# Windowed attention and a gated expert on one core: h by Strassen's algorithm from the fourth chunk on

## The chip, the core and the metric

The kernel runs on one core of a Trainium2 chip. A core has five engines with queues of their own: PE (TensorE, matrix multiplication), DVE (VectorE), ACT (ScalarE), POOL (GpSimd) and SP (SyncE, which here issues nearly all DMA transfers). The profile shows PE's weight loads apart, as PEld. The metric is the time of one execution on the device in microseconds (us).

## The reference

What is computed is an attention with a mask, whose result goes through an expert with a gate:

```python
scores = scale * np.matmul(q, k.transpose(0, 1, 3, 2))      # batch 8, 8 heads, 576 positions, 64 wide
# heads 0-3: the last 32 positions; heads 4-7: every fourth of the last 128
scores = np.where(masks[None, :, :, :], scores, -1000000000.0)
attn = np.exp(scores - np.max(scores, axis=-1, keepdims=True))
attn = attn / (np.sum(attn, axis=-1, keepdims=True) + 1e-09)
x = np.matmul(attn, v)                                     # then as 4608 tokens x 512

h = x @ w_in                                               # 512 -> 2048
sp = np.maximum(h, 0.0) + np.log1p(np.exp(-np.abs(h)))
g = h * erf(sp)
out = g @ w_out                                            # 2048 -> 512
```

The weights come as numbers of 64 bits. The kernel splits each factor of the two expert products into a high and a low part of 32 bits (type fp32r), and forms every product as three: high x high, high x low, low x high.

## The kernel before, in words

**Attention** works on 72 units of 256 queries by two heads. A unit is visited twice: its scores, mask and maximum at one visit; three units later its transposes (`turn`), its product with the values (`values`) and the writing of its rows as high and low part (`rows_hi` on ACT, `rows_lo` on DVE). Finished rows go to DRAM tiles `xT` and come back as chunks. The first 14 units run alone, the others beside the expert.

**The expert** takes the 4608 tokens in nine chunks of 512 (0 to 8), and h in pairs of 128 columns. A step t (of 72) is a pair in a chunk; 8 steps make a chunk, only chunk 0 is worked in two halves around chunk 1. A step is two half-steps, x = 2t + j, with j 0 or 1. In each, `mm1` makes 128 columns of h for the chunk's 512 tokens: 12 matmuls (4 parts of the 512 inner numbers, three products each) of a 128x128 weight by 512 tokens, into one PSUM bank `h`. DVE copies the bank to `hc` (`take`, L492). When both columns of a pair are there, ACT computes the argument (sigmoid and logarithm, `argument`) and a half-step later erf (`table`); DVE multiplies and splits g into `ghi` and `glo` (`gate`, j = 0 for the product and the first half, j = 1 a half-step later for the second). `mm2` for the step two back, 12 matmuls of 512 columns into four PSUM banks `acc`, stands on PE behind each `mm1`.

**The order** is written by hand: the loop over x at the end of the kernel issues everything, and no scheduler moves it. On PE a half-step is: the transposes of a visit if there is one, `mm1`, `mm2`, then values and scores of the visit. On DVE: `take`, copies of transposes, normalizing, `gate`, mask and maximum, `rows_lo`. `visits()` is the table that says at which x which units are visited; from unit 30 on they come in twos. SP issues DMAs strictly in the order of the program, and an issue that waits holds up those behind it. PSUM is full: `h`, two banks for scores and transposes (`sp`), one (`tx`) for the values' products and four `acc`.

**SBUF** holds both parts of both weights for the whole run (`win_hi`, `win_lo`, `wout_hi`, `wout_lo`), made in the first half-steps; four tiles `xs` hold a chunk's x, with two of the staging tiles `dbl` in turn with them for every second chunk.

Of the kernel before, what the change touches and what calls it, by code (L numbers as in the profile page):

```python
# [10 lines left out]
F32 = mybir.dt.float32  # L11
# [7 lines left out]
P = 128  # L19
# [54 lines left out]


def visits():
# [12 lines left out]
    return at  # L89
# [39 lines left out]
def attn_moe_kernel(ctx: ExitStack, tc: tile.TileContext, qk, v, masks, eye, w_in, w_out, out):  # L129
# [15 lines left out]

    win_hi = wpool.tile([P, CC, DF], F32R, name="win_hi")
    win_lo = wpool.tile([P, CC, DF], F32R, name="win_lo")
    wout_hi = wpool.tile([P, FT, DM], F32R, name="wout_hi")
# [9 lines left out]
    vz = [one.tile([P, SIDE, 2, D], F32, name=f"v{i}") for i in range(2)]  # L158
    pz = [one.tile([P, TOK], F32, name=f"pT{i}") for i in range(2)]

# [8 lines left out]
    def place(u, p):  # L169


        if u < FREE:
            return acc[(u + 1 + 2 * p) % 4][:, p * P:(p + 1) * P]
        at = p * PARTS * P + (u in second) * P
        return (spb[1] if p else bank)[:, at:at + P]

# [187 lines left out]
    for g in range(DF // TOK):  # L364
        cs = slice(g * TOK, (g + 1) * TOK)
        for c in range(CC):
            prep.append((USED[2 * g], w_in[c, g], win_hi[:, c, cs], win_lo[:, c, cs]))
    for f in range(FT):
# [23 lines left out]
    def load_w(i):  # L392
        if prep:
# [3 lines left out]
            staged.append((i, d, hi, lo))  # L397

    calls = [0]

    def prep_act():


        calls[0] += 1
        if made:
            w, hi, lo = made.popleft()
            nc.scalar.copy(out=hi, in_=w)
            rest.append((calls[0], w, hi, lo))
        if staged:
            i, d, hi, lo = staged.popleft()  # L410
            w = io.tile([P, TOK], F32, name="w", bufs=4)
            nc.scalar.activation(out=w, in_=d[:, :, 1].bitcast(F32), func=AF.Abs, scale=REBASE)
            begun.append((calls[0], i, d, hi, lo, w))

    def prep_dve(keep=None):
# [3 lines left out]
        if rest and rest[0][0] < calls[0]:  # L419
            _, w, hi, lo = rest.popleft()  # L420
            nc.vector.tensor_tensor(lo, w, hi.bitcast(F32), op=ALU.subtract)  # L421
        if begun and begun[0][0] < calls[0]:
# [51 lines left out]
    def mm1(t, j):  # L474
# [7 lines left out]
        for k, cc in enumerate(ccs):  # L482
            for i, (w, x) in enumerate(((win_hi, hi), (win_hi, lo), (win_lo, hi))):
                nc.tensor.matmul(h, w[:, cc, ft * P:(ft + 1) * P], x[cc],  # L484
                                 start=(k == 0 and i == 0), stop=(k == CC - 1 and i == 2))

    hs, ls, gs = {}, {}, {}
# [79 lines left out]
    with tc.manual_schedule():  # L567
# [25 lines left out]
        for x in range(2 * (NT + 2)):  # L593
# [8 lines left out]
            if t < NT:  # L602
                after = STEPS[t + 1][0] if ends(t) and t + 1 < NT else None
                if x == 2 * HALF - 4:
                    load_x(1, range(twice))
                elif after and after > 1 and j == 0:
# [3 lines left out]
                mm1(t, j)  # L610
                if x == 0:
                    for a in stores:
                        store_x(*a)
                if after is not None and j == PAIR - 1:
                    load_x(after, range(twice, CC))
                    hold(False)
                take(t, j)

# [130 lines left out]
```

## Time and profile before

| | |
|---|---|
| median of 3 runs | 926.96 us (926.67 to 928.45) |
| profiled execution, first to last instruction | 924.6 us |
| PE busy | 895.2 us, 97% |
| PE matmuls | 8208, each with its own weight load |
| DVE, ACT, POOL busy | 561.4, 638.2, 75.4 us |
| moved by DMA | 103.66 MB, mean 112 GB/s |
| chunk 3's first half-step (x = 48) starts | 345.3 us |
| chunk 8's last half-step of h starts | 903.9 us |

The span is 2.4 us under the median of the runs. A row of groups reads: line, engine, operation, what is written <- what is read, shapes, count, then total busy time and the mean of one in ns, then the idle time of the engine ahead of it with what ended it. A row of the timeline reads: start, duration, engine, line, operation, tiles, count. The end of a matmul is modelled, so its pace is read from starts.

### The profile page before, as it was taken

To read this page: it belongs to the slowest core of one execution; us is meant where nothing else is said; L and a number is where in the kernel's file an instruction comes from. 1 tells how busy PE (TensorE), PEld (TensorE's weight loads), DVE (VectorE), ACT (ScalarE), POOL (GpSimd) and SP (SyncE) were. 2 spreads that over 40 slices of the span, in tenths; PEclk is the share of its full clock that TensorE was granted. 3 is DMA by queue.
4 is the path that set the end of the run, shared out by engine and by line. 5 is a ranking of instruction groups with operands and counts; after the bars stand their busy time and mean duration, and the time that the engine had idled before them with its cause. 6 is when DMAs were issued, how large, how long until landed. Compare 5 with 4: busy or idle time off the path is not lost.

```text
span 924.6 us, 20394 instructions
## 1 busy us (share of the span) xinstructions
PE 895.2 (97%) x8208; PEld 730.8 (79%) x8208; DVE 561.4 (61%) x1633; ACT 638.2 (69%) x1266; POOL 75.4 (8%) x92
## 2 busy tenths in 40 slices
PE   4689999999999999999999999999999999999998
PEld 3467877888888888888888888888888888888886
DVE  6879989886566655555566555555655444445444
ACT  7779988885866866766678675877676554455553
POOL 2211100000001100000000010000000000000000
PEclk9999999999999999999999999999999999999999
DMA  8885544532632252324233263233311311011001
GB/s 300 271 280 186 170 161 141 164 120 92 213 119 73 75 170 81 108 74 145 71 118 100 71 216 100 95 103 111 120 50 38 117 51 41 1 45 46 1 1 45
DMA packets 53823, 103.66 MB, mean 112 GB/s; under 512 B 7136, under 2 KB 20192, under 8 KB 53728
## 3 DMA queue, kind: packets, MB, share of 16 engines
q1 hardware_dynamic: 53440, 101.83, 33.0%
q8 instruction: 64, 1.05, 0.5%
q10 hardware_dynamic: 288, 0.52, 0.1%
q14 instruction: 31, 0.25, 0.1%
HBM read 74.15 MB, written 27.26 MB: 110 GB/s over the span
## 4 chain that ended last, share of the span: by engine, by line
PE 90%; DVE 5%; ACT 2%; DMA 2%; issue 1%; SPq 0%; POOL 0%; DVEq 0%; ACTq 0%
PE h L484 42%; PE acc L525 40%; PE tx L262 3%; PE sp L204 3%; PE sp L243 1%; DMA dbl<-in_w_in_dram 1%; DVE w L426 1%; DVE w L427 1%; DMA qk<-in_qk_dram 1%; PE sp L262 1%; DVE win_lo L421 1%; DVE prob L215 0%; DVE w L425 0%; DVE s L507 0%; DVE x L309 0%
## 5 line engine op out<-in xcount | busy, mean ns | idle before, releaser
L492 DVE COPY hc<-h 128x512 f32<-128x512 f32 x144 | 99.4, 691 | 273.1 <-PE h L484 273.0
L484 PE MATMUL h<-x,win_hi 128*128 128x512 f32 x832 | 260.7, 395 | 2.1 <-DVE hc L492 1.9
L525 PE MATMUL acc<-wout_hi,ghi 128*128 128x512 f32 x576 | 227.6, 395 | 0.4 <-DVE ghi L510 0.2
L525 PE MATMUL acc<-wout_lo,ghi 128*128 128x512 f32 x576 | 224.6, 390 | 0.0
L496 ACT ACTIVATE s<-hc 128x1024 f32<-128x1024 f32 x72 | 76.4, 1062 | 185.2 <-DVE hc L492 185.0
L484 PEld LDWEIGHTS h<-x,win_hi 128*128 128x128 f32 x832 | 156.1, 189 | 35.7 <-DVE hc L492 2.5
L484 PE MATMUL h<-x,win_lo 128*128 128x512 f32 x416 | 163.5, 393 | 0.0
L525 PE MATMUL acc<-wout_hi,glo 128*128 128x512 f32 x576 | 159.0, 389 | 0.0
L525 PEld LDWEIGHTS acc<-wout_hi,glo 128*128 128x128 f32 x576 | 108.1, 188 | 23.0
L525 PEld LDWEIGHTS acc<-wout_hi,ghi 128*128 128x128 f32 x576 | 108.2, 188 | 22.8 <-DVE ghi L510 0.6
L525 PEld LDWEIGHTS acc<-wout_lo,ghi 128*128 128x128 f32 x576 | 108.2, 188 | 21.6
L238 POOL TENSOR_TENSOR prob<-prob,rinv 128x256 f32<-128x256 f32 x72 | 70.9, 995 | 578.6 <-DVE ssum L236 282.6
L511 DVE TENSOR_TENSOR glo<-s,ghi 128x512 fp32r<-128x512 f32 x144 | 100.1, 695 | 5.1
L225 ACT ACTIVATE prob<-prob,nmax 128x64 f32<-128x64 f32 x288 | 96.4, 338 | 3.1 <-DVE nmax L215 2.7
L507 DVE TENSOR_TENSOR s<-hc,s 128x1024 f32<-128x1024 f32 x72 | 93.5, 1299 | 5.4 <-ACT s L500 5.4
L497 ACT ACT_TABLE_LOAD x72 | 92.4, 1283 | 1.3
L500 ACT ACT_TABLE_LOAD x72 | 92.4, 1283 | 1.3
L484 PEld LDWEIGHTS h<-x,win_lo 128*128 128x128 f32 x416 | 78.8, 189 | 17.0
L215 DVE CUSTOM_DVE_ANT_0 prob<-sp,cst 128x64 f32<-128x64 f32 x288 | 47.1, 220 | 56.9 <-PE sp L204 47.0
L484 PE MATMUL h<-dbl,win_hi 128*128 128x512 f32 x256 | 80.6, 396 | 0.0
L500 ACT ACTIVATE s<-s 128x1024 f32<-128x1024 f32 x72 | 76.4, 1062 | 0.8
L497 ACT ACTIVATE s<-s 128x1024 f32<-128x1024 f32 x72 | 76.4, 1061 | 0.8
(61 smaller groups left out, 922.5 us busy)
## 6 DMA issues: line engine op xcount, KB each, us to landing
v<-in_v_dram SPq DMA_DIRECT2D x72, 256.0 KB, 4.1
xT<-rows SPq DMA_DIRECT2D x26, 576.0 KB, 4.8
qk<-in_qk_dram SPq DMA_DIRECT2D x48, 272.0 KB, 3.8
dbl<-in_w_in_dram SPq DMA_DIRECT2D x16, 512.0 KB, 4.3
dbl<-in_w_out_dram SPq DMA_DIRECT2D x16, 512.0 KB, 3.6
qk<-in_qk_dram SPq DMA_DIRECT2D x24, 288.0 KB, 4.0
out_dram<-w SPq DMA_DIRECT2D x26, 256.0 KB, 2.3
x<-xT SPq DMA_DIRECT2D x8, 320.0 KB, 5.3
```

Source lines behind the costliest of these rows:

```text
L215: nc.vector.tensor_tensor_reduce(out=pr[:, g, :], in0=sps[h][:, u % 2, p, :], in1=mask[QUADS.index(kinds(u, p))], scale=-SCALE, scalar=BIG ...
L225: nc.scalar.activation(out=probs[u][:, j, :], in_=probs[u][:, j, :], func=AF.Exp, scale=-1.0, bias=nmax[:, j:j + 1], accum_out=sums[u][:, ...
L238: nc.gpsimd.tensor_tensor(probs[u], probs[u], rinv.broadcast_to([P, 2 * PARTS, KEYS]), op=ALU.mult)
L262: nc.tensor.matmul(xp[h * D:(h + 1) * D, qs], vt[ks, s, h, :], pt[ks, h * P + s * STRIP:h * P + (s + 1) * STRIP], start=True, stop=True, t ...
L484: nc.tensor.matmul(h, w[:, cc, ft * P:(ft + 1) * P], x[cc], start=(k == 0 and i == 0), stop=(k == CC - 1 and i == 2))
L492: nc.vector.tensor_copy(out=hs[t][:, j], in_=h)
L496: nc.scalar.activation(out=ls[t], in_=hs[t], func=AF.Sigmoid, scale=-1.0)
L497: nc.scalar.activation(out=ls[t], in_=ls[t], func=AF.Ln, bias=TINY)
L500: nc.scalar.activation(out=ls[t], in_=ls[t], func=AF.Erf, scale=-1.0)
L507: nc.vector.tensor_tensor(out=e, in0=hc, in1=e, op=ALU.mult)
L511: nc.vector.tensor_tensor(out=glo, in0=e[:, j], in1=ghi.bitcast(F32), op=ALU.subtract)
L525: nc.tensor.matmul(acc[tt], g[:, tt * P:(tt + 1) * P], w[:, ft, :], start=(first and w is wout_hi and g is ghi), stop=(last and g is glo))
```

## The change

Chunks 0 to 2 stay as they are. From chunk 3 on (`FAST = 3`) a step's pair of columns is no longer two times 12 matmuls of 512 tokens. The step is seen as a product of 2x2 blocks: the pair's weights, 2 x 128 columns by 512 inner numbers, are A11, A12, A21, A22 (column by half of the inner numbers), the chunk's x is B11, B12, B21, B22 (half of the inner numbers by half of the 512 tokens). Strassen's algorithm in Winograd's form gets the four blocks of h from 7 block products where 8 are usual. A block product is 2 parts of 128 inner numbers by the same three products of high and low, so 6 matmuls, each of 256 tokens. A step has 42 of these in place of 24 of 512.

- **Sums of weights.** Three of the left factors are A11, A12, A22, four are sums S1 to S4. In half-steps 31 to 48 `build` makes them, one pair of columns every two half-steps: a sum of the high and low part on DVE (`sum_whole`), four sums on POOL (`sum_parts`), high parts on ACT, low parts on DVE, and all seven factors go to a DRAM tile `ws`. They are never built again; the SBUF of the old weights is free once chunk 2 is through.
- **Streaming.** `load_left` brings the seven factors of the next step back, 4 in the half-step j = 0 (1.05 MB) and 3 in j = 1 (0.79 MB), into one of two places in the SBUF of the old weights.
- **Sums of x.** Seven half-steps ahead of a chunk `right_load` loads its four blocks; DVE adds their parts (`right_whole`, L592), POOL makes T1 to T4 (L598), ACT casts their high part (L603, in the last half-step but one before the chunk) and DVE makes the low part (L608, in the last).
- **On PE** `mm1_fast` makes products 0 to 3 in j = 0 (24 matmuls) and 4 to 6 in j = 1 (18). They go to halves of two banks: `h`, and `tx`, which the values' products leave; these move into the `sp` banks.
- **Taking h** (`take_fast`) is three operations of DVE in j = 0 (256, 512, 256 columns) and two in j = 1 (512 each), which add the products up.
- **Visits** come at other half-steps: every second one from 31 to 37, then so that a chunk's rows are through before its load; the last is at 104 (before: 109). From 47 on they are at 47, 52, 56, 59, 62, 65, 68, 72, 76, 79, 84, 88, 91, 94, 97, 100, 104.

The diff, cut:

```diff
+FAST = 3
+HN = TOK // 2
+KIND = 2 * 2 * P
+LEFT = ("A11", "S3", "A12", "S2", "S1", "S4", "A22")
+PART = 4
+RIGHT = ("B11", "T3", "B21", "T2", "T1", "B22", "T4")
+PLACES = (1, 0), (1, 1), (0, 0), (0, 1), (1, 0), (0, 0), (0, 1)
+BUILD = 2 * SPC * 2 - 1
+READY = 7
+ANCHORS = [(0, 31), (1, 33), (2, 35), (3, 37), (4, 40), (8, 56), (13, 72), (17, 88), (22, 104)]
...
-        x = 2 * SPC + 15 + 32 * k // 9
+        x = paced(k)
...
+    ws = dram.tile([SPC, P, len(LEFT) * KIND], F32, name="ws")
+    stages, sums_of, cells, wholes = {}, {}, {}, {}
+    def sum_whole(p):
+        r = sums_of[p] = doubles(2).bitcast(F32).rearrange("p n w -> p (n w)") if p % 2 else plain
+        a = win_at[:, p].rearrange("p j k i c n -> p (j k) i (c n)").bitcast(F32)
+        nc.vector.tensor_tensor(out=r.rearrange("p (b n) -> p b n", b=4), in0=a[:, :, 0], in1=a[:, :, 1], op=ALU.add)
+        for name in ("A11", "A12", "A22"):
+            b, n = LEFT.index(name), 2 * int(name[1]) + int(name[2]) - 3
+            src = win[:, (4 * p + n) * KIND:(4 * p + n + 1) * KIND].bitcast(F32)
+            nc.sync.dma_start(out=ws[p][:, b * KIND:(b + 1) * KIND], in_=src)
+    def sum_parts(p):
+        a11, a12, a21, a22 = (sums_of[p][:, i * HN:(i + 1) * HN] for i in range(4))
+        nc.gpsimd.tensor_tensor(out=a22, in0=a21, in1=a22, op=ALU.add)
+        nc.gpsimd.tensor_tensor(out=a21, in0=a11, in1=a21, op=ALU.subtract)
+        nc.gpsimd.tensor_tensor(out=a11, in0=a22, in1=a11, op=ALU.subtract)
+        nc.gpsimd.tensor_tensor(out=a12, in0=a12, in1=a11, op=ALU.subtract)
+    def sum_hi(p):
+        tiles = [xs[i][:, n, 0:KIND] for i in range(2) for n in range(2)]
+        stages[p] = list(zip(("S2", "S4", "S3", "S1"), tiles))
+        for i, (_, t) in enumerate(stages[p]):
+            nc.scalar.copy(out=t[:, 0:HN], in_=sums_of[p][:, i * HN:(i + 1) * HN])
+    def sum_lo(p):
+        r = sums_of.pop(p)
+        for i, (name, t) in enumerate(stages.pop(p)):
+            b = LEFT.index(name)
+            nc.vector.tensor_tensor(out=t[:, HN:KIND], in0=r[:, i * HN:(i + 1) * HN], in1=t[:, 0:HN].bitcast(F32),
+                                    op=ALU.subtract)
+            nc.sync.dma_start(out=ws[p][:, b * KIND:(b + 1) * KIND], in_=t.bitcast(F32))
+    def build(x):
+        for k, stage in ((3, sum_lo), (2, sum_hi), (1, sum_parts), (0, sum_whole)):
+            p, odd = divmod(x - BUILD - k, 2)
+            if not odd and 0 <= p < SPC:
+                stage(p)
+    def load_left(t, j):
+        if t < NT and STEPS[t][0] >= FAST:
+            at = slice(0, PART * KIND) if j == 0 else slice(PART * KIND, len(LEFT) * KIND)
+            nc.sync.dma_start(out=left(t).bitcast(F32)[:, at], in_=ws[STEPS[t][1]][:, at])
...
+    def right_whole(c):
+        o = cells[c]
+        for name in ("B12", "B11", "B22", "B21"):
+            w = wholes[name] = io.tile([P, TOK], F32, name="w", bufs=4)
+            a = o[name].bitcast(F32)
+            nc.vector.tensor_tensor(out=w, in0=a[:, 0], in1=a[:, 1], op=ALU.add)
+    def right_parts(c):
+        w11, w12, w21, w22 = (wholes.pop(name) for name in ("B11", "B12", "B21", "B22"))
+        for out, a, b in ((w11, w12, w11), (w12, w22, w12), (w22, w22, w11), (w21, w21, w22)):
+            nc.gpsimd.tensor_tensor(out=out, in0=a, in1=b, op=ALU.subtract)
+        wholes.update(T1=w11, T2=w22, T3=w12, T4=w21)
+    def right_hi(c):
+        for name, w in wholes.items():
+            nc.scalar.copy(out=cells[c][name][:, 0], in_=w)
+    def right_lo(c):
+        for name in list(wholes):
+            t = cells[c][name]
+            nc.vector.tensor_tensor(out=t[:, 1], in0=wholes.pop(name), in1=t[:, 0].bitcast(F32), op=ALU.subtract)
+    def right(x):
+        c, at = divmod(x + READY, 2 * SPC)
+        if FAST <= c < NCH:
+            if at == 0:
+                right_load(c)
+            elif at == 2:
+                right_whole(c)
+            elif at == 3:
+                right_parts(c)
+            elif at == 5:
+                right_hi(c)
+            elif at == 6:
+                right_lo(c)
+    def mm1_fast(t, j):
+        o, w = cells[STEPS[t][0]], left(t).rearrange("p (b i c n) -> p b i c n", b=len(LEFT), i=2, c=2)
+        for k in range(PART) if j == 0 else range(PART, len(LEFT)):
+            (b, half), x = PLACES[k], o[RIGHT[k]].rearrange("p i (c n) -> p i c n", c=2)
+            for c in range(2):
+                for n, (wi, xi) in enumerate(((0, 0), (0, 1), (1, 0))):
+                    nc.tensor.matmul((h, bank)[b][:, half * HN:(half + 1) * HN], w[:, k, wi, c, :], x[:, xi, c, :],
+                                     start=(c == 0 and n == 0), stop=(c == 1 and n == 2))
+    def take_fast(t, j):
+        if j == 0:
+            hs[t], ls[t] = (work.tile([P, PAIR, TOK], F32, name=n) for n in ("hc", "s"))
+        a = hs[t].rearrange("p f (k n) -> p (f k) n", k=2)
+        x, y = (q.rearrange("p (k n) -> p k n", k=2) for q in (h, bank))
+        if j == 0:
+            nc.vector.tensor_copy(out=a[:, 2], in_=y[:, 0])
+            nc.vector.tensor_tensor(out=a[:, 0:2], in0=x, in1=a[:, 2:3].broadcast_to([P, 2, HN]), op=ALU.add)
+            nc.vector.tensor_tensor(out=a[:, 2], in0=y[:, 1], in1=a[:, 1], op=ALU.add)
+        else:
+            nc.vector.tensor_tensor(out=a[:, 1::2], in0=y[:, 0:1].broadcast_to([P, 2, HN]), in1=a[:, 1:3], op=ALU.add)
+            nc.vector.tensor_tensor(out=a[:, 1:3], in0=x, in1=a[:, 1:3], op=ALU.add)
...
+                fast = STEPS[t][0] >= FAST
+                (mm1_fast if fast else mm1)(t, j)
...
-                take(t, j)
+                (take_fast if fast else take)(t, j)
...
             if t >= 2:
                 attend(ready, scored)
+            load_left(t + 1, j)
+            right(x)
+            build(x)
```

What this makes of the engines' order shows best at the start of chunk 8, where no visit is near. On **DVE**, the last half-step of a chunk before the change, and the one behind it (L492 takes h; L507, L510, L511 are the gate):

```order
L492 COPY hc<-h 128x512
L507 TENSOR_TENSOR s<-hc,s 128x1024
L510 CAST ghi<-s 128x512
L511 TENSOR_TENSOR glo<-s,ghi 128x512
L492 COPY hc<-h 128x512
```

and now, the last half-step of chunk 7 and the first of chunk 8 (L644 and L645 take h, L667 to L671 are the gate, L640 to L642 take the next):

```order
L644 TENSOR_TENSOR hc<-tx,hc 128x2x256
L645 TENSOR_TENSOR hc<-h,hc 128x512
L667 TENSOR_TENSOR s<-hc,s 128x1024
L670 CAST ghi<-s 128x512
L671 TENSOR_TENSOR glo<-s,ghi 128x512
L608 TENSOR_TENSOR dbl_9765<-w,dbl_9765 128x512
L608 TENSOR_TENSOR x_100<-w,x_100 128x512
L608 TENSOR_TENSOR x_98<-w,x_98 128x512
L608 TENSOR_TENSOR win<-w,win 128x512
L640 COPY hc<-tx 128x256
L641 TENSOR_TENSOR hc<-h,hc 128x512
L642 TENSOR_TENSOR hc<-tx,hc 128x256
```

The four L608 are the low parts of T1, T2, T3 (`x_98`) and T4. They stand behind the gate, and the taking of the new chunk's first h stands behind them. On **PE**, at the same place, the last of chunk 7's output and the first block of chunk 8:

```order
L685 MATMUL acc_95<-wout_hi,glo 128x512
L685 MATMUL acc_96<-wout_hi,glo 128x512
L631 MATMUL tx<-x_97,win 128x256 x6
L631 MATMUL tx<-x_98,win 128x256 x6
L631 MATMUL h<-x_99,win 128x256 x6
L631 MATMUL h<-x_100,win 128x256 x6
L685 MATMUL acc_93<-wout_hi,ghi 128x512
```

Before, twelve matmuls of 512 columns stood there. The second group of six reads T3 (`x_98`), the third of the four that DVE makes. On **SP**, behind a visit (L208 and L212 bring q, k and v of two units to come, L350 stores finished rows), the next streamed load of weights (L560):

```order
L208 DMA qk_83<-in_qk_dram 128x544
L212 DMA v_86<-in_v_dram 128x512
L208 DMA qk_84<-in_qk_dram 128x544
L212 DMA v_85<-in_v_dram 128x512
L350 DMA xT_106<-rows 128x1152
L560 DMA win<-ws 128x2048
```

Before, the same first five rows stood there, and behind them at most the loads of a chunk's x or the stores of its output.

More of the change, by code (lines that the diff above doesn't have):

```diff
@@ L158, in attn_moe_kernel @@
     vz = [one.tile([P, SIDE, 2, D], F32, name=f"v{i}") for i in range(2)]
-    pz = [one.tile([P, TOK], F32, name=f"pT{i}") for i in range(2)]
+    pz = [one.tile([P, n], F32, name=f"pT{i}") for i, n in enumerate((2 * P, TOK))]
+    plain = one.tile([P, 2 * TOK], F32, name="plain")
     spb = [ps.tile([P, TOK], F32, name=f"sp{i}") for i in range(2)]
@@ L364, in attn_moe_kernel @@
     for g in range(DF // TOK):
-        cs = slice(g * TOK, (g + 1) * TOK)
         for c in range(CC):
-            prep.append((USED[2 * g], w_in[c, g], win_hi[:, c, cs], win_lo[:, c, cs]))
+            hi, lo = (win_at[:, 2 * g:2 * g + 2, :, c // 2, i, c % 2, :] for i in range(2))
+            prep.append((USED[2 * g], w_in[c, g], hi, lo))
     for f in range(FT):
@@ L406, in prep_act @@
             w, hi, lo = made.popleft()
-            nc.scalar.copy(out=hi, in_=w)
+            nc.scalar.copy(out=hi, in_=like(w, hi))
             rest.append((calls[0], w, hi, lo))
@@ L614, in attn_moe_kernel @@
                 if after is not None and j == PAIR - 1:
-                    load_x(after, range(twice, CC))
+                    if after < FAST:
+                        load_x(after, range(twice, CC))
                     hold(False)
-                take(t, j)
+                (take_fast if fast else take)(t, j)
             if x == 1 or j == 0 and x:
```

49 lines of the change are left out of this document (40 added, 9 removed).

## The prediction

> **What bounds the kernel now.** I read the page's busy shares first, then a table of stretches, then the chain of waits, and last single matmuls, the DVE and the DMA issues in order of time.
>
> ```profile
> PE 895.2 (97%) x8208; PEld 730.8 (79%) x8208; DVE 561.4 (61%) x1633; ACT 638.2 (69%) x1266; POOL 75.4 (8%) x92
> ```
>
> ```profile
> 100.00:200.00 100.00, 99.04 (x857) 80.64 (x856) 87.92 (x216) 84.98 (x153) 6.09 (x6) 1.00 0.45 150
> 345.00:690.00 345.00, 345.00 (x3361) 284.02 (x3349) 199.20 (x641) 242.01 (x493) 31.99 (x30) 1.00 0.32 105
> 690.00:904.00 214.00, 214.00 (x1035) 176.78 (x1034) 96.76 (x158) 119.70 (x130) 2.03 (x2) 1.00 0.11 37
> ```
>
> The columns are the stretch, then busy time of PE, PEld, DVE, ACT and POOL, granted clock, DMA share and GB/s. The change works in the last two rows (its first half-step starts at 345 us) and prepares in the stretch before. There PE has no idle time at all and the clock is full, so only PE time counts, as long as DVE (58% and 45%), ACT (70% and 56%) and DMA stay out of the way. The chain shows the same: nothing but matmuls.
>
> ```profile
> 751.75 2.72 PE h L484 x12
> 754.47 2.72 PE acc L525 x12
> 757.18 2.72 PE h L484 x12
> ```
>
> Twelve matmuls of 512 columns take 2.72 us: one each 226.7 ns, for h as for the output. A half-step x is one block of h and one of output, 5.44 us; a step t is two.
>
> **What the change takes off PE.** Per step 24 matmuls of 512 columns become 42 of 256, in 48 steps (chunks 3 to 8). The 24 cost 24 x 0.2267 = 5.44 us. The price of a short one stands nowhere in the trace, so it is bounded. From below: half of 226.7, 113.3 ns. The weight load could hold it higher, so I looked where loads stand alone:
>
> ```profile
> 701.36 0.30 PEld L484 LDWEIGHTS h<-dbl,win_hi 128*128 128x128 f32 x2
> 701.70 0.19 PEld L484 LDWEIGHTS h<-dbl,win_lo 128*128 128x128 f32 x1
> 720.54 0.38 PE L243 MATMUL sp<-ident,prob 128*128 128x128 f32 x2
> 49.93 1.05 PE L484 MATMUL h<-x,win_hi 128*128 128x512 f32 x2
> 50.78 0.63 PE L484 MATMUL h<-x,win_lo 128*128 128x512 f32 x1
> ```
>
> After a pause two loads of 0.19 us end 0.30 us after the first began, so they start 0.11 us apart. Two transposes with their loads (mean 273 ns) cover 0.38 us: also 0.11 apart. So a load and its matmul can follow each other every 110 ns, just under 113.3. The last two rows are from the first half-step of the expert part: there two matmuls take 0.85 us, 0.425 each, nearly twice 213 ns. At the later pace each takes 13 ns more than 213. Such a rest can be a fixed price of each matmul; then 256 columns take 106.7 + 13.3 = 120 ns. It can also grow with the columns; then they take 113.3. I take **120 ns**, since the rest is missing in the slow rows, where something that runs beside the array would be hidden. 42 x 0.120 = 5.04 us, a gain of 0.40 us a step and **19.2 us** in all; with 113.3 ns it is 4.76 and 32.6 us. From above: at 129.5 ns nothing is left.
>
> The Trainium skill, "TensorE: Matmul & The Clock Gate", section "Back-to-back issue gap", gives N/2.4 + 2.5 ns, so 215.8 for 512 and 109.2 for 256 columns; the row has 226.7 for the first, so the page is 11 ns short here. By its figures the gain would be 48 x (24 x 0.2158 - 42 x 0.1092) = 28 us, an estimate.
>
> **DVE at the start of a chunk.** This is the price I find on the path. The new chunk's T1 to T4 get their second halves (L608) in the half-step before the chunk, behind that half-step's gate. T3 is third of the four, and the new chunk's eighth matmul needs it.
>
> ```profile
> 661.95 0.69 DVE L492 COPY hc<-h 128x512 f32<-128x512 f32 x1 [0.48 <-PE h L484]
> 662.56 1.22 DVE L507 TENSOR_TENSOR s<-hc,s 128x1024 f32<-128x1024 f32 x1
> 663.81 0.43 DVE L510 CAST ghi<-s 128x512 fp32r<-128x512 f32 x1
> 664.27 0.69 DVE L511 TENSOR_TENSOR glo<-s,ghi 128x512 fp32r<-128x512 f32 x1
> 664.88 0.68 DVE L563 COPY dbl<-acc 128x512 f32<-128x512 f32 x1
> ```
>
> Start to start, an operation on 512 takes 0.61 us and the gate 1.25 + 0.46 + 0.61 = 2.32. Let T be the start of DVE's copy, 0.2 us after h is finished. *No visit near* (chunks 7 and 8): the last of the copies ends at T + 0.61, the gate at 2.93, T3 at 2.93 + 3 x 0.61 + 0.1 = 4.9. PE has only 2.72 us of output and seven matmuls (0.84) from T - 0.2, so it arrives at T + 3.4. It waits 1.5 us, twice: 3.0.
>
> ```profile
> 610.69 0.69 DVE L492 COPY hc<-h 128x512 f32<-128x512 f32 x1 [3.69 <-PE h L484]
> 611.30 0.75 DVE L247 COPY pT<-sp 128x256 f32<-128x256 f32 x2
> 611.96 1.22 DVE L507 TENSOR_TENSOR s<-hc,s 128x1024 f32<-128x1024 f32 x1
> 615.74 0.23 DVE L215 CUSTOM_DVE_ANT_0 prob<-sp,cst 128x64 f32<-128x64 f32 x1 [1.37 <-PE sp L204]
> 624.76 0.16 DVE L236 TENSOR_SCALAR ssum<-ssum 128x4 f32<-128x4 f32 x1
> 625.39 1.61 DVE L507 TENSOR_TENSOR s<-hc,s 128x1024 f32<-128x1024 f32 x1
> ```
>
> *A visit in that half-step* (47 and 79, before chunks 3 and 5) adds 0.66 us of copies and 0.63 of normalizing to DVE, but PE is longer busy too: its scores end at T + 5.0. DVE then has T3 at 4.9 + 1.3 = 6.2, PE arrives at 5.0 + 0.84 = 5.8. Waits 0.4 us, twice: 0.8. *A visit one half-step earlier* (62 and 94, before chunks 4 and 6): now ACT is late, since the four new casts (L603) stand between the rows of the visit and the erf for which the gate waits.
>
> ```profile
> 653.97 0.69 DVE L492 COPY hc<-h 128x512 f32<-128x512 f32 x1 [1.12 <-PE h L484]
> 658.97 0.23 DVE L215 CUSTOM_DVE_ANT_0 prob<-sp,cst 128x64 f32<-128x64 f32 x1 [2.59 <-PE sp L204]
> 659.33 0.28 ACT L304 CAST rows<-sp 128x128 fp32r<-128x128 f32 x1
> 659.63 1.28 ACT L500 ACT_TABLE_LOAD   x1
> 660.93 1.06 ACT L500 ACTIVATE s<-s 128x1024 f32<-128x1024 f32 x1
> L407 ACT CAST win_hi<-w 128x512 fp32r<-128x512 f32 x16 | 9.8, 613 | 0.7 <-DVE w L427 0.6
> ```
>
> From T at 653.97 the rows end at 5.6; four casts (613 ns each, I take 0.5 since neighbours overlap by a tenth) bring 7.6, table and erf 10.0, the gate 12.3, T3 14.2. PE: scores at 5.0, then 18 x 0.12 + 2.72 + 0.84, so 10.7. It waits 3.5 us, twice: 7.0. Together **10.8 us**; from 3 (ACT and DVE run ahead of my chain) to 16.
>
> **Other work of DVE, ACT and POOL.** Taking h costs three and two operations instead of two in all (0.36 + 0.61 + 0.36, and 2 x 0.61, half of a 512 each where 256): about 2.5 us a step for 1.2. PE needs the banks again after a block of output, 2.72 us later: hidden, with 1.2 us to spare. The sums of a chunk (L592, 4 x 0.61) fall into visits at 59 and 91; there DVE is late by about 0.5 us each: 1.0. In half-steps 31 to 48 the sums of weights add, per step, 1.25 + 4 x 0.35 us to DVE (2.65), four casts to ACT (1.3) and four operations to POOL. With a visit each step DVE has 4.6 + 3.8 + 2.65 = 11 us of PE's 2 x 5.44 + 2.4 = 13.3. POOL makes DVE slower where both run:
>
> ```profile
> 600.96 2.17 POOL L238 TENSOR_TENSOR prob<-prob,rinv 128x256 f32<-128x256 f32 x2 [11.32 <-DVE ssum L236]
> 601.04 1.61 DVE L507 TENSOR_TENSOR s<-hc,s 128x1024 f32<-128x1024 f32 x1
> ```
>
> 1.61 us against 1.22 without POOL: a third more on 4.3 us, 1.4, and 12.4 of 13.3 is still under. I take 2 us for queues that do not fit, 0 to 6.
>
> **The stream from DRAM.** Per step 7 x 512 x 4 x 128 bytes = 1.84 MB. Full queues move about 325 GB/s:
>
> ```profile
> 618.00:620.00 2.00, 2.00 (x10) 1.64 (x10) 1.97 (x8) 2.00 (x13) 0.00 (x0) 1.00 1.00 370
> 620.00:622.00 2.00, 2.00 (x11) 1.65 (x10) 0.62 (x1) 1.98 (x6) 0.00 (x0) 1.00 0.98 313
> 622.00:624.00 2.00, 2.00 (x11) 1.65 (x10) 0.00 (x0) 1.08 (x2) 0.00 (x0) 1.00 0.97 293
> ```
>
> So 5.6 us of 10.5, a share of 0.54 on top of the 0.32 above. The tight place is behind a visit. SP then issues q, k, v of two units (1.08 MB) from T + 5, the rows' store (0.58), which waits for DVE, and behind it the next load (1.05): 2.7 MB, 8.3 us, plus some 2 until it is seen: T + 15.3. It is needed two blocks of h later, at T + 5.0 + 5.6 + 4.9 = 15.5. It just fits. I take 1 us, 0 to 8. PE's own pace does not suffer: in these rows ten or eleven matmuls start in 2 us, under full DMA load.
>
> **Sum.** -19.2 + 10.8 + 1.0 + 2 + 1 = **-4.4 us**. The profiled span of 924.6 becomes 920.2. The median of the runs, 926.96, stands 2.4 above that span: **922.6 us**.
>
> **Rivals.** *Half the columns, half the time* (113.3 ns): the h blocks in the fast chunks take 32.6 us less and the waits stay: -32.6 + 14.8 = -17.8, 909 us. For it: 110 ns is what loads and transposes already reach. Against it: the 13 ns that the slow rows lack. *A short matmul is held by its own weights* (slower): each needs a load of its own, and only 256 columns hide it. With waits of 14.8 us the change loses from 5.44 - 14.8/48 = 5.13 us a step, that is from 122 ns a matmul. At 130 ns it is 14.8 us slower, 942. For it: after each pause the matmuls stay longer for a while:
>
> ```profile
> 616.21 0.40 PE L484 MATMUL h<-x,win_lo 128*128 128x512 f32 x1
> 618.29 0.39 PE L484 MATMUL h<-x,win_lo 128*128 128x512 f32 x1
> ```
>
> Between these two lie nine matmuls in 2.08 us, 231 ns each instead of 226.7, though their loads are long done. Against it: loads 0.11 us apart. *Loads that come late* (slower): if behind each of the 17 visits from half-step 47 on the next load is 2 us late, 34 us replace my 1: 955 us. For it: the 0.2 us of room. Against: four of five half-steps have no visit, and the queues empty there. *Loads that do not overlap at all*: at the recorded 0.19 us each, 42 would take 8.0 us where 5.04 is assumed: 2.9 x 48 = 141 more, some 1,064 us. The first load row above speaks against it, two loads in 0.30 us. The Trainium skill, "Perfetto Trace Analysis", section "Identifying the Most-Contended Engine", would have one judge PE by the busy share of LDWEIGHTS; that is 79% here and by the recorded length would pass 100% (66 loads of 0.19 us are 12.5 us in a step of 10.5), so the rule speaks against the change. The trace differs in that the records overlap. That the change would not do what it says I leave out: the order has the 42 short matmuls in all 48 steps.
>
> **How the numbers follow.** My sum (120 ns) gets 50%, with a range of its own of 914 to 932 from the bounds of the waits; 113.3 ns 25%; held by its weights 17%; late loads 5%; loads that do not overlap 3%. The range of 907 to 938 reaches to the middle of the 113.3 case and to break-even and half of the 130 ns case, and leaves about 2 in 10 out. About 0.2%, 1.9 us, is what a measurement of this kernel can tell from no change. My sum is only 2.5 us beyond that, so of its 50% I count 31 as faster, 8 as the same, 11 as slower; the 113.3 case is faster but for 1, the others slower but for 2: faster 0.55, the same 0.11, slower 0.34.
>
> **What would show it.** (1) Start to start of the 256-column matmuls in chunk 8, without visits: 120 ns if my sum holds, 113 or 130 for the rivals. (2) Twelve of 512 still in 2.72 us. (3) PE idle ahead of L631 with DVE L608 as releaser, six times, the two longest near 3.5 us, before chunks 4 and 6. (4) Little idle time ahead of L631 with the DMA of ws as releaser: over 8 us in all would make the late loads right. (5) No PE idle time worth the name in half-steps 31 to 46. The prediction is wrong if (1) is off by more than 5 ns, which is 10 us, or if the waits of (3) are under 3 or over 16 us.

## The result and the profile after

| | us |
|---|---|
| before, median of 4 runs beside it | 927.71 (926.67 to 928.92) |
| after, median of 4 runs | 969.82 (966.94 to 971.45) |
| ratio | 1.045 (95% interval 1.043 to 1.047) |
| forecast | 922.6, range 907 to 938 |
| profiled execution after: time, span | 969.75, 968.0 |
| start of half-step 48; of the last half-step of h (x = 143) | 354.9; 947.7 |

The change makes the kernel 42 us slower. The forecast was wrong in sign, and its range does not hold the time.

The busy shares and the row of granted clock on the page of after:

```profile
PE 898.0 (93%) x9072; PEld 771.6 (80%) x9072; DVE 696.3 (72%) x1865; ACT 656.3 (68%) x1322; POOL 135.4 (14%) x148
PEclk9999999999999899999999999988999999999999
```

The same stretches as for before (columns as there, stretch, PE, PEld, DVE, ACT, POOL, granted clock, DMA share, GB/s):

```profile
100.00:200.00 100.00, 98.80 (x856) 80.31 (x855) 87.50 (x216) 84.32 (x155) 6.10 (x6) 1.00 0.44 146
355.00:690.00 335.00, 312.12 (x3513) 278.64 (x3513) 235.37 (x688) 225.63 (x474) 46.38 (x40) 0.96 0.66 238
690.00:948.00 258.00, 244.17 (x1581) 219.63 (x1581) 163.49 (x279) 141.15 (x154) 13.96 (x10) 0.98 0.55 194
```

Up to 200 us little differs (PE is busy for 98.80 us of the first stretch, 99.04 before). Behind 355 us, where before PE was busy all the time, it now stands idle for 335 - 312.1 + 258 - 244.2 = 36.7 us, and the clock is no longer full. No other engine took its place: DVE, ACT and DMA are at 70%, 67% and 66% in the middle stretch. What holds PE is a row of waits. The waits of PE, longest first (what waits, for what, us in total, times, longest):

```profile
PE tx L631 <- DMA win<-ws: 22.7, 11, 3.8
PE tx L631 <- DVE x L608: 8.7, 3, 3.7
PE sp L224 <- DMA qk<-in_qk_dram: 7.5, 5, 3.5
PE acc L282 <- ACT pT L267: 6.0, 6, 1.2
PE sp L282 <- DVE pT L267: 4.9, 2, 3.8
PE tx L631 <- DVE win L608: 4.3, 3, 1.7
```

The wait for qk lies at the kernel's start. The waits for ws, for L608 and the 3.8 of pT are new.

**The matmuls do what was forecast.** PE in chunk 8, in order of time:

```profile
916.18 0.88 PE L631 MATMUL tx<-dbl,win 128*128 128x256 f32 x6
916.90 0.88 PE L631 MATMUL h<-dbl,win 128*128 128x256 f32 x6
917.62 0.88 PE L631 MATMUL h<-win 128*128 128x256 f32 x6
918.34 0.40 PE L685 MATMUL acc<-wout_hi,ghi 128*128 128x512 f32 x1
921.08 1.59 PE L631 MATMUL tx<-x,win 128*128 128x256 f32 x12
```

Six start 0.72 us apart: 120 ns each. Half-steps without a wait last 5.62 us (j = 0) and 4.90 (j = 1), so a step takes 10.52 where 10.88 stood: 0.36 x 48 = 17.3 us gained. All the loss is in half-steps that last longer. I took the start of each half-step from the first matmul of `mm1` and subtracted what its like lasts without a wait. From 31 on that makes four groups: starts of chunks (x = 48, 64, 80, 96, 112, 128) 19.3 us; half-steps 4 and 5 of every chunk (from 52 on) 19.6; the half-steps 58, 59, 75, 76, 90 to 92 and 107 around the loading and summing of x 14.3; 37, 44 and 45 in the build 7.7. Together 60.9, and 60.9 - 17.3 = 43.6 us; the spans differ by 43.4.

**Half-steps 4 and 5.** SP's queue and then PE, ahead of half-step 133 (L725 stores the chunk's output, L560 is the stream):

```profile
837.70 28.66 SPq L560 DMA_DIRECT2D win<-ws  x6
885.10 0.34 SPq L725 DMA_DIRECT2D out_dram<-dbl  x1
886.12 1.31 SPq L725 DMA_DIRECT2D out_dram<-w  x3
887.53 2.20 SPq L560 DMA_DIRECT2D win<-ws  x4
```

```profile
888.72 1.07 PE L685 MATMUL acc<-wout_hi,glo 128*128 128x512 f32 x4
893.57 1.12 PE L631 MATMUL tx<-dbl,win 128*128 128x256 f32 x6 [3.77 <-DMA win<-ws]
894.49 1.48 PE L631 MATMUL h<-dbl,win 128*128 128x256 f32 x6
```

From 866.4 (837.70 + 28.66) to 885.1 SP issues nothing. It stands at the first output store, which waits for DVE's copy; the loads of ws behind it are issued when the stores are through, four at once, and PE waits 3.77 us for the first.

**Starts of chunks.** DVE ahead of chunk 4, and PE:

```profile
454.44 1.23 DVE L667 TENSOR_TENSOR s<-hc,s 128x1024 f32<-128x1024 f32 x1 [1.12 <-ACT s L660]
456.77 0.68 DVE L608 TENSOR_TENSOR dbl<-w,dbl 128x512 fp32r<-128x512 f32 x1
457.37 1.28 DVE L608 TENSOR_TENSOR x<-w,x 128x512 fp32r<-128x512 f32 x2
458.58 0.68 DVE L608 TENSOR_TENSOR win<-w,win 128x512 fp32r<-128x512 f32 x1
```

```profile
454.04 0.99 PE L631 MATMUL tx<-x,win 128*128 128x256 f32 x7
458.71 1.44 PE L631 MATMUL tx<-x,win 128*128 128x256 f32 x5 [3.69 <-DVE x L608]
459.95 2.76 PE L631 MATMUL h<-x,win 128*128 128x256 f32 x12
```

As forecast: seven matmuls, then the wait for T3, behind a gate that waited for ACT's erf. What was not forecast is the last row: behind the pause the twelve matmuls of h take 2.56 us (459.95 to 462.51, where the next output begins), 213 ns each, not 120.

**The clock.** In the stretches behind the pause at 893.57:

```profile
893.57:895.80 2.23, 2.23 (x13) 2.23 (x14) 0.69 (x1) 0.00 (x0) 0.00 (x0) 0.63 1.00 420
895.80:898.00 2.20, 2.20 (x11) 2.02 (x11) 0.71 (x2) 0.00 (x0) 0.00 (x0) 0.60 1.01 427
898.00:900.00 2.00, 2.00 (x10) 1.67 (x9) 1.93 (x3) 1.97 (x2) 0.00 (x0) 1.00 0.93 350
```

The granted clock is down for 3.4 us in the midst of it. The trace has nine such stretches of 3.41 or 6.83 us from 300 us to the end of the matmuls, eight at or just behind a pause of PE of 2.5 us or more, one behind a pause of 1.7.

### The profile page after: what moved, and what is told of

The parts are those of the page before. It is cut to its first block, busy times and chain, and to the rows that moved or that the text cites. A ratio compares the mean times of both kernels' runs of the same rounds, so it can differ in the third digit from the quotient of the medians.

```text
span 968.0 us, 22988 instructions
## 1 busy us (share of the span) xinstructions
PE 898.0 (93%) x9072; PEld 771.6 (80%) x9072; DVE 696.3 (72%) x1865; ACT 656.3 (68%) x1322; POOL 135.4 (14%) x148
## 4 chain that ended last, share of the span: by engine, by line
PE 63%; DVE 14%; DMA 10%; ACT 7%; issue 2%; SPq 2%; POOL 0%; DVEq 0%; ACTq 0%
PE acc L685 27%; PE h L631 12%; PE h L508 10%; PE tx L631 9%; DMA win<-ws 6%; PE sp L282 2%; DVE s L667 2%; PE sp L224 2%; DMA x<-xT 2%; DVE prob L235 1%; DVE ghi L670 1%; SPq L583 1%; ACT s L656 1%; ACT s L657 1%; DVE w L450 1%
## 5 line engine op out<-in xcount | busy, mean ns | idle before, releaser
L685 PE MATMUL acc<-wout_hi,ghi 128*128 128x512 f32 x576 | 230.5, 400 | 0.4 <-DVE ghi L670 0.2
L685 PE MATMUL acc<-wout_lo,ghi 128*128 128x512 f32 x576 | 226.9, 394 | 0.0
L685 PEld LDWEIGHTS acc<-wout_hi,ghi 128*128 128x128 f32 x576 | 110.3, 192 | 21.4 <-DVE ghi L670 0.6
L685 PEld LDWEIGHTS acc<-wout_lo,ghi 128*128 128x128 f32 x576 | 109.7, 190 | 19.6
L671 DVE TENSOR_TENSOR glo<-s,ghi 128x512 fp32r<-128x512 f32 x144 | 104.4, 725 | 5.1
L631 PE MATMUL h<-win 128*128 128x256 f32 x720 | 101.7, 290 | 0.0
L508 PE MATMUL h<-x,win 128*128 128x512 f32 x384 | 98.5, 399 | 2.1 <-DVE hc L652 2.1
L667 DVE TENSOR_TENSOR s<-hc,s 128x1024 f32<-128x1024 f32 x72 | 92.0, 1278 | 11.3 <-ACT s L660 11.3
L631 PEld LDWEIGHTS h<-win 128*128 128x128 f32 x720 | 95.3, 199 | 0.0
L324 ACT CAST rows<-sp 128x128 fp32r<-128x128 f32 (+7 forms) x167 | 27.6, 303 | 97.9 <-PE sp L224 88.2
L508 PEld LDWEIGHTS h<-x,win 128*128 128x128 f32 x384 | 73.1, 192 | 18.3 <-DVE hc L652 2.5
L235 DVE CUSTOM_DVE_ANT_0 prob<-sp,cst 128x64 f32<-128x64 f32 x288 | 45.5, 219 | 45.6 <-ACT rows L324 30.7
L631 PE MATMUL tx<-win 128*128 128x256 f32 x432 | 63.4, 292 | 15.4 <-DMA win<-ws 10.3
```

Source lines behind the costliest of these rows:

```text
L235: nc.vector.tensor_tensor_reduce(out=pr[:, g, :], in0=sps[h][:, u % 2, p, :], in1=mask[QUADS.index(kinds(u, p))], scale=-SCALE, scalar=BIG ...
L324: nc.scalar.copy(out=hi, in_=src)
L508: nc.tensor.matmul(h, win_at[:, ftp, j, cc // 2, w, cc % 2, :], x[cc], start=(k == 0 and i == 0), stop=(k == CC - 1 and i == 2))
L631: nc.tensor.matmul((h, bank)[b][:, half * HN:(half + 1) * HN], w[:, k, wi, c, :], x[:, xi, c, :], start=(c == 0 and n == 0), stop=(c == 1 ...
L667: nc.vector.tensor_tensor(out=e, in0=hc, in1=e, op=ALU.mult)
L671: nc.vector.tensor_tensor(out=glo, in0=e[:, j], in1=ghi.bitcast(F32), op=ALU.subtract)
```

## The experiments

**Does a short matmul cost 120 ns apart from the stream? (halves)** The kernel before, no Strassen:

```diff
-        for k, cc in enumerate(ccs):
-            for i, (w, x) in enumerate(...):
-                nc.tensor.matmul(h, w[:, cc, ...], x[cc], ...)
+        for a in (0, TOK // 2) if c >= 3 else (0,):
+            n = TOK // 2 if c >= 3 else TOK
+            for k, cc in enumerate(ccs):
+                for i, (w, x) in enumerate(...):
+                    nc.tensor.matmul(h[:, a:a + n], w[:, cc, ...], x[cc][:, a:a + n], ...)
```

> The kernel before with each matmul of mm1 from the fourth chunk on split in two of 256 columns: 24 in place of 12 in each half-step, the same sums and waits, no Strassen. It measures the price of a short matmul apart from the stream. A fixed part of 13.3 ns in each matmul (120 ns for 256 columns against 226.7 for 512): 48 steps x 24 further matmuls x 13.3 ns = +15.3 us, so 941 to 945. Rival, time in proportion to columns (113.3 ns): 0, so 927 to 929. Rival, held by the load of its own weights (130 ns): 48 x (48 x 0.130 - 24 x 0.2267) = +38 us, so about 966.

Measured: 945.45 us, half a microsecond above the range; before 926.16 beside it, ratio 1.0208 (1.0192 to 1.0223): +19.3. One block of h, and the first output matmul behind it:

```profile
804.77 0.40 PE L486 MATMUL h<-x,win_hi 128*128 128x256 f32 x2
805.00 0.28 PE L486 MATMUL h<-x,win_lo 128*128 128x256 f32 x1
807.64 0.40 PE L527 MATMUL acc<-wout_hi,ghi 128*128 128x512 f32 x1
```

From 804.77 to 807.64 are 24 matmuls, 120 ns each. 24 x 48 more matmuls of 13.3 ns are 15.4 us of the 19.3. By half-steps it is 0.18 us each where no visit is near and 0.12 to 0.13 with a visit or right behind one; 24 matmuls of 120 ns for 12 of 226.7 make 0.16. The starts of chunks 7 and 8 hold 1.7 and 1.2 us more, and half-step 47 1.4. 256 further columns cost 106.7 ns (226.7 - 120), so 13.3 ns of each matmul are fixed here, and both rivals on its price fall.

**Are the loads late because of their place? (lead, ahead)** Two ways to get the stream out from behind the stores:

```diff
-            load_left(t + 1, j)
+            load_left(t + 2, j)        # lead, in the same place

+                load_left(t + 1, j)    # ahead: in front of mm1, and not behind the stores
                 fast = STEPS[t][0] >= FAST
```

> The changed kernel with each load of weight sums asked for four half-steps ahead of its use in place of two (load_left(t + 2, j) for load_left(t + 1, j)); nothing else moves. Theory (the loads are late because they stand in SP's queue behind the four output stores of a chunk, which wait for DVE and ACT copies, and behind the chunk's 8 to 12 loads of x): the waits of L631 for DMA win<-ws go from 37.5 us to under 5, the half-clock stretches behind them (half-steps 69, 101, 117, 133) go too, and the time falls from 970 to between 940 and 952. Rival one (the DMA engines are too busy while a chunk's stores, loads of x and the stream meet, so that more lead is used up by the same bytes): the waits for ws shrink by less than half and the time stays at 958 to 970. Rival two (the wait only moves: with ws on time PE waits for DVE or ACT in the same half-steps): the row for ws vanishes, rows for DVE grow by as much, 965 to 970.

> The changed kernel with load_left(t + 1, j) at the head of its half-step, ahead of the half-step's own matmuls, output stores and loads of x, in place of behind them; the lead stays two half-steps. It changes only the place in SP's queue. Theory (place behind the stores makes the loads late): the waits at half-steps 4 and 5 of each chunk (19.6 us) go, those around the loads of x, which stand in the half-step before, stay in part: 948 to 958. Rival (bandwidth, or a lead too short in itself): 966 to 971.

Measured: lead 939.1 (ratio 1.0145, 1.0124 to 1.0165), 30.7 us less than after and just under its range. Ahead 947.66 (1.0231, 1.0216 to 1.0246), 22.2 less, just under its range too. The 37.5 us of waits for ws that lead's expectation starts from are wrong: the list of after has 22.7. The first waits of PE in lead, and the first in ahead:

```profile
PE sp L224 <- DMA qk<-in_qk_dram: 10.9, 8, 3.6
PE tx L631 <- DVE x L608: 8.7, 3, 3.7
```

```profile
PE tx L631 <- DMA win<-ws: 9.3, 7, 3.9
PE sp L224 <- DMA qk<-in_qk_dram: 8.9, 5, 3.6
PE tx L631 <- DVE x L608: 8.7, 3, 3.7
```

In lead no wait for ws is left; in ahead, with the lead unchanged, 9.3 us of the 22.7. Half-steps 116, 117, 132 and 133 went from 9.51, 6.32, 9.56 and 6.48 us to 5.62, 4.90, 5.62 and 4.90 in lead, and within 0.04 of that in ahead. What ahead keeps lies mostly where the loads of x hold SP (59, 75, 76, 91, 107), as here in after:

```profile
522.32 0.43 SPq L560 DMA_DIRECT2D win<-ws  x1
522.79 9.87 SPq L583 DMA_DIRECT2D win<-xT  x12
532.71 1.55 SPq L560 DMA_DIRECT2D win<-ws  x3
```

There is bandwidth enough: with the same bytes, asked for earlier, no wait for ws is left. The place in the queue was the cause: ahead changes nothing else.

**The starts of chunks (early).**

```diff
-            elif at == 5:
+            elif at == 4:
                 right_hi(c)
-            elif at == 6:
+            elif at == 5:
                 right_lo(c)
```

> The changed kernel with right_hi and right_lo one half-step earlier each (at 4 and 5 of right's count in place of 5 and 6), so that the low parts of T1 to T4 are formed two half-steps ahead of their chunk. Theory (PE waits at each start of a chunk for L608, queued on DVE behind the gate and made late by ACT's casts): the excess at half-steps 48, 64, 80, 96, 112 and 128 falls from 19.3 us in all to under 4, with it the two half-clock stretches inside 64 and 96, and the time from 970 to between 948 and 955. Rival (DVE is short of time, so that the four subtractions push the gate instead, and PE waits for ghi and glo at mm2): under 8 us gained, 962 to 970, with waits of mm2's matmuls on DVE in their place.

Measured: 955.41 (949.93 to 963.13; ratio 1.0297, 1.0263 to 1.0331), 14.4 us less, just above its range. The six half-steps last 5.62 to 5.72 us, and no wait for L608 is left. The gain is short of 19.3 by 5: the time is given back in part at 47 and 49 (2.1 and 1.5 us more), and in the profiled execution, 7.7 us above the median, 101, 107, 108 and 117 last 1.0 to 1.5 us longer than in after.

**Both together, and a version that is faster than before (both, shift, spread, late, moved).**

> The edits of lead and early together. Theory (the two causes are separate places in the schedule): the gains add, 969.8 - 30.7 - 14.4 = 924.7, so 921 to 929 beside a kernel before of 926 to 928, and the waits of L631 for ws and for L608 are both gone. Rival (one pause hides the other, or early's subtractions now collide with the gate on DVE): 930 to 939.

Measured: 924.98 us, before 927.34 beside it, ratio 0.9972 (0.9957 to 0.9986). The gains add to within 2 us (924.7 by the sum of the times, 926.6 by the sum of the ratios), and two small moves of the order turn a loss of 4.5% into a gain of 0.3%. In both the longest pause left is at half-step 44. DVE there, then POOL and PE:

```profile
325.09 3.60 DVE L592 TENSOR_TENSOR w<-win 128x512 f32<-128x512 f32 x4 [1.41 <-DMA win<-xT]
328.61 2.28 DVE L518 TENSOR_TENSOR plain<-win 128x1024 f32<-128x1024 f32 x1
330.82 0.68 DVE L652 COPY hc<-h 128x512 f32<-128x512 f32 x1
331.42 0.74 DVE L267 COPY pT<-sp 128x256 f32<-128x256 f32 x2
```

```profile
326.46 5.55 POOL L598 TENSOR_TENSOR w<-w 128x512 f32<-128x512 f32 x3 [3.33 <-DMA ws<-x]
331.88 2.25 PE L282 MATMUL sp<-pT,v 64*64 64x32 f32 x64 [3.72 <-DVE pT L267]
```

The sums of x and of weights stand ahead of the copies of pT for a visit, and two of them are slow: three of the four L592 last 0.68 us and one 1.78, and L518 lasts 2.28. Each of these two started while POOL was in an L598, and ended 0.5 and 1.1 us behind the end of that L598; without POOL at work beside them, L592 lasts 0.68 to 0.69 us and L518 1.21 to 1.22. I first tried to form all sums of x earlier (shift), and with it the last sums of weights later (spread):

```diff
-READY = 7
+READY = 8
...
-            load_left(t + 1, j)
-            right(x)
+            load_left(t + 2, j)
...
             for m in ready:
                 rows_lo(m)
+            right(x)
```

```diff
             p, odd = divmod(x - BUILD - k, 2)
-            if not odd and 0 <= p < SPC:
+            p -= p > 5
+            if not odd and 0 <= p < SPC and x - BUILD - k != 12:
```

> lead, and all five steps on the sums of x one half-step earlier (READY = 8, called at the end of the half-step so that the loads follow the stores of x that they need), so that L608 is two half-steps ahead of its chunk as in early, and the four sums of L592 are no longer ahead of the copies of pT for the visits at 44, 60 and 76. Theory: as both, and the pause at half-step 76 (3.8 us in lead) and those at 59, 60 and 92 (1.3 each) go as well: 916 to 921. Rival (DVE is late by its whole load there, not by the order): no better than both, 922 to 930.

> shift, and the sums of weights of the last two pairs of columns (p of 6 and 7) formed two half-steps later each, after the fourth chunk's sums of x instead of among them. Theory (the pause of 5.4 us at half-step 44 and its half clock at 45 come of L518, L542, L592 and L598 of both builds falling into two half-steps): the pause falls under 2 us, 5 to 6 us less than shift: 911 to 916. Rival (the pause is the wait of L592 for the loads of x, which stays): as shift within 1.5 us.

Measured: 944.67 (1.0168, 1.0141 to 1.0196) and 940.55 (1.0145, 1.0104 to 1.0186): some 20 and 16 us slower than both, and far outside what theory and rival had. A row of DVE's waits in shift says why:

```profile
DVE w L592 <- DMA win<-xT: 13.3, 3, 5.9
```

The loads of x now stand in the half-step of a visit, behind the store of its rows, and when DVE comes to the sums two half-steps later they have not landed. DVE waits for them in order, and behind it everything that PE waits for: half-steps 43, 59 and 91 last 10.48, 12.11 and 10.63 us where both has 5.44, 7.28 and 7.28. My expectation counted the work on DVE and not the landing of the loads. So the sums of x stay where they were, and what collides with them moves: the last two sums of weights (late, the second diff above on both), and besides five visits (moved):

```diff
+MOVED = {44: 45, 47: 49, 52: 53, 76: 77, 79: 81}
...
         x = paced(k)
+        x -= x % (2 * SPC) == 0
+        x = MOVED.get(x, x)
```

> both, and the sums of weights of the last two pairs of columns (p of 6 and 7) formed two half-steps later each, so that they no longer fall among the fourth chunk's sums of x; the sums of x stay where both has them, behind loads that have landed. In both the half-steps 44, 45 and 47 last 13.11, 6.56 and 10.08 us against 7.88, 5.59 and 7.88. Theory (too much of both builds in DVE's and POOL's queues ahead of the visit at 44): 5 to 8 us of these 8.4 go, 917 to 920. Rival (the wait of L592 for the loads of x, 1.4 us, and POOL's slowing of L592 make it alone): under 2.5 us gained, 922.5 to 925.

> late, and five of the visits one or two half-steps later (44 to 45, 47 to 49, 52 to 53, 76 to 77, 79 to 81), so that no copies of pT stand right behind the four sums of L592 at 43 and 75. Theory (the sums of x hold DVE for 3.6 us ahead of the copies of pT for the next half-step's visit): the rest of the pause at 44 and the 3.8 us at 76 with its traces at 77 and 79 go too, 4 to 7 us less than late: 911 to 916. Rival (the visit meets other work of DVE and POOL wherever it stands): within 2 us of late.

Measured: late 919.48 (0.9924, 0.9909 to 0.9939), moved 917.11 (0.9882, 0.9865 to 0.9899), before 926.93 beside both. Late gains 5.5 us on both (4.4 by the ratios); half-steps 44, 45 and 47 last 9.53, 7.01 and 8.60. Moved takes another 2.4 (3.9 by the ratios), less than the 4 to 7 that I expected. At 76 there was less to gain: I had set its 9.43 us against 5.62, but a half-step with a visit lasts 8.00, so 1.4 were lost there and not 3.8. With the visit in 77 it is 6.93, still 1.3 too long, and 37, 44, 60 and 92 keep 0.9 to 1.8 us each. Moved is 1.2% faster than the kernel before, and behind half-step 104 (from 690 us) PE has no idle time:

```profile
690.00:897.00 207.00, 207.00 (x1329) 187.20 (x1328) 139.04 (x220) 119.63 (x114) 11.78 (x8) 1.00 0.58 195
```

**What halves the clock? (pauses)** Moved, with idle sums on DVE that make PE pause where few transfers run:

```diff
+DELAY = {55: 5, 57: 4, 59: 6, 61: 7, 66: 8, 68: 9, 70: 12}
...
+            for _ in range(DELAY.get(t, 0)):
+                nc.vector.tensor_tensor(out=plain[:, 0:TOK], in0=plain[:, 0:TOK], in1=plain[:, TOK:2 * TOK], op=ALU.add)
```

> moved, with idle sums on DVE (0.61 us each; they add one half of a tile that is no longer used to the other) ahead of its taking of h in seven steps of the last three chunks, where there are no visits and few transfers: 5, 4, 6, 7, 8, 9 and 12 of them. PE has about 1.2 us to spare there, so it should pause for about 1.9, 1.2, 2.5, 3.1, 3.7, 4.3 and 6.1 us. Theory (a pause of over some 3.4 us is followed by a stretch of half clock, whatever else runs): full clock behind the first three pauses, half clock for 3 to 7 us behind the last three, the fourth (3.1) open; each stretch costs about 1.5 us beside the pause itself. Rival (the half clock comes of the full DMA queues in which the pauses of the changed kernel stood): full clock behind all seven. The time: 917.1 and the pauses' 23 us, and 4 to 6 more by the theory: 940 to 948.

Measured in one run: 933.66 us, under the 940 to 948 expected. The half-steps grew by 1.1, 0, 1.1, 1.5, 3.4, 2.9 and 5.1 us, less than I meant, since PE had some 2 us to spare and not 1.2. Two of the pauses and the stretches behind them:

```profile
846.21:849.43 3.22, 0.01 (x2) 0.00 (x1) 3.01 (x7) 0.00 (x0) 0.00 (x0) 1.00 1.00 347
849.43:852.84 3.41, 3.41 (x24) 3.19 (x24) 2.62 (x5) 0.24 (x1) 0.00 (x0) 1.00 0.37 147
894.76:899.68 4.92, 0.00 (x1) 0.00 (x0) 4.65 (x9) 0.00 (x0) 0.00 (x0) 0.97 0.00 0
899.68:902.76 3.08, 3.08 (x14) 3.08 (x15) 1.66 (x3) 0.00 (x0) 0.00 (x0) 0.50 0.00 0
```

The pause of 3.22 us under full queues is followed by full clock, the one of 4.92 us with no transfer at all by half clock, and the half-step behind it lasts 6.35 us for 4.90: 1.45 more. So full queues are not needed for it, and a pause is enough. The limit is not one length: 3.2 and 2.7 us had no such effect here, while 3.1, 2.5 and once 1.7 us had it in after (those that end at 643.2, 708.7 and 494.1 us). The Trainium skill, "TensorE: Matmul & The Clock Gate", section "What's actually happening", says that activity is judged in windows of 3413 ns that run free of the kernel. The traces agree: in each of the twelve the granted clock changes only on one grid of 3.413 us, and the grid lies differently in each run. On it the pause of 3.22 us is split over two windows, with PE idle for 1.93 us in one and 1.29 in the next, and the one of 4.92 us fills a whole window:

```profile
844.73:848.14 3.41, 1.48 (x7) 0.91 (x5) 3.25 (x6) 0.65 (x1) 0.00 (x0) 1.00 1.04 316
848.14:851.56 3.42, 2.13 (x18) 2.13 (x18) 2.83 (x5) 0.00 (x0) 0.00 (x0) 1.00 0.70 292
895.93:899.34 3.41, 0.00 (x0) 0.00 (x0) 3.20 (x6) 0.00 (x0) 0.00 (x0) 1.00 0.00 0
```

I counted the windows at full clock behind 300 us in all twelve traces. Each of the 30 in which PE was idle for 2.08 us or more was followed by half clock, of the 11 with 1.5 to 1.93 us four were, and of the other 2,123 one. So what counts is how much of one window a pause takes. That is a count over pauses as they came: no run moves one and the same pause against the grid, and what decides between 1.5 and 1.93 us stays open.

## Why the prediction was wrong

1. **Price of a short matmul: right.** 120 ns, in the trace and in halves. The gain is 17.3 us and not 19.2: the two half-steps of a step last 0.04 us longer together than 42 x 0.120 and two blocks of output.
2. **Start of a chunk: the mechanism right, the size wrong.** All six waits came, released by L608. The pause before chunk 4 is 3.69 us by the trace, forecast 3.5. But the term was 10.8 and the half-steps held 19.3 us. Early removed 14.4. The six waits alone are 13.0 us (8.7 + 4.3 in the list); before chunks 3 and 5 they are 1.3 and 1.7 where I had 0.4. What the sum lacked for the rest is that a pause lowers the clock: half-steps 64 and 96 lose 6.3 us each for pauses of 3.7. My sum priced a pause at its own length; it costs about 1.5 us more where 3.41 us of half clock follow, and 2.7 at these two, where 6.83 follow. The Trainium skill, "TensorE: Matmul & The Clock Gate", section "HAM oscillation — how this bites in real kernels", describes waits that drop the gate again and again; nine stretches of half clock in after agree, though the pauses here are 1.7 to 3.8 us long. I had read the page for the gap between matmuls and not for this.
3. **The stream: the step that failed.** "The tight place is behind a visit": I followed one load behind q, k, v and the rows' store, found that it just fits, and took 1 us. Behind visits it does fit: half-steps 56, 62, 72, 88 and 94, each with a visit, last 8.00 us in after as in lead. The tight place is elsewhere in the same queue: behind the four output stores of each chunk, which wait for DVE's and ACT's copies, and behind the 8 to 12 loads of x. From there PE waits 22.7 us for ws, where my sign for late loads was 8. Asking earlier removed 30.7 us. This term alone turns the forecast's gain into a loss: -4.4 - 1 + 30.7 is 25 us slower. I had listed what SP issues at a visit, and not what it issues in the half-steps where a chunk ends or is loaded. The rival of late loads had 34 us, close to it by luck: it had them behind the 17 visits, the wrong places, and 5% of the chances.
4. **Sums and build: too small.** 2 us for the build, measured 7.7, and PE pauses for 3.8 us in half-step 44, where I had said that nothing worth the name would be seen up to 46. Late took 4.6 us off half-steps 44, 45 and 47. L592 was to cost 0.5 us each at 59 and 91, and costs 1.2 to 1.4 at each of 60, 76 and 92 in lead. POOL was to make DVE a third slower, and the two sums above last 1.78 and 2.28 us for 0.68 and 1.22. I took DVE's work of a whole step against PE's time. The trace shows the order within: the chunk's sums and the pair's sums stand directly ahead of the copies for a visit.
5. **The rest.** That the stream does not slow matmuls was right: ten start between 898 and 900 us with the queues at 0.93. The rivals on the price of a matmul, 113.3 and 130 ns, are out, and so are weight loads that do not overlap (in chunk 8 loads recorded at 0.19 us start 0.12 us apart).

By terms, forecast and measured: matmuls -19.2 and -17.3; starts of chunks 10.8 and 19.3; sums of x and the stream 2 and 33.9 (19.6 + 14.3); build 2 and 7.7. Sum -4.4 and +43.6, against 42.1 by the medians. I spent 45 of 100 chances and the lower half of the range on the price of a matmul; what decided was the queue, which had 5%.

## What to carry to other kernels

A transfer that is added to a queue issued in order waits with whatever stands ahead of it (here SP stood for 18.7 us at one output store, 866.4 to 885.1), so list every issue of that queue over a whole period of the loop, with what each waits for, before its bandwidth is counted; and ask for it one period earlier where space allows. A pause of the matmul engine of 2 us or more is priced with the half clock that may follow (here 1.5 us for each 3.41), and several small waits that look hidden on average are to be followed in their order on the engine. An algorithm with fewer multiplications paid here (0.9882) only when each of its transfers and sums had its own place in the schedule.

## What was not expected of the hardware

- The granted clock falls to 0.50 for 3.41 or 6.83 us behind a pause, and 256-column matmuls are then 213 ns apart and not 120; in moved, without such pauses, the clock of the whole profiled run is 1.00, in after 0.977. The idle time within one window of a fixed grid of 3.413 us tells whether it comes: always from 2.08 us on, almost never below 1.5.
- Matmuls keep their 120 ns pace under DMA queues at 0.93 to 1.00, also when their weights have just come from DRAM (after, both, moved).
- Twelve loads of x (L583) take SP 9.1 to 10.2 us to issue in after, eight 7.7 and 5.1 (9.87 us for twelve at 522.79, with the queues full), so a load behind them starts that much later.
- A sum on DVE that starts while POOL is in one of its sums of x (L598) ends 0.5 to 1.1 us behind the end of that one: L592 in 1.78 us for 0.68, L518 in 2.28 for 1.22.
